# Cluster maxima of a routing-attention kernel kept in spare columns of the values' PSUM bank

## The chip, the cores and the metric

The kernel runs on one core of one Trainium2 chip. The metric is the device time of one execution in microseconds (us), as the median of the runs shown. TensorE, VectorE, ScalarE, GpSimd and SyncE appear in the profile as PE (PEld for its weight loads), DVE, ACT, POOL and SP.

## The reference

Four batches of eight heads, 768 tokens each, head width 64. Every query and key goes to the nearest of 16 centroids of its head, and a query attends only to keys with the same cluster. The result, 3072 rows of 512, passes through a feed-forward block with a softmax-gated unit and a normalisation.

```python
q_assign = np.argmax(np.einsum('bhsd,hcd->bhsc', q_n, c_n), axis=-1)
k_assign = np.argmax(np.einsum('bhsd,hcd->bhsc', k_n, c_n), axis=-1)
mask = q_assign[:, :, :, None] == k_assign[:, :, None, :]
scores = np.where(mask, scale * np.matmul(q, k.transpose(0, 1, 3, 2)), -1e9)
attn = softmax(scores)                       # with 1e-9 in the divisor
x = np.matmul(attn, v)                       # heads side by side: (3072, 512)
h = x @ w_in                                 # (3072, 1024)
solu = h * softmax(h)
out = (layernorm(solu) * g_ln) @ w_out       # (3072, 512)
```

The part that the change touches is the argmax: the maximum of 16 products per token, and the comparison with it that gives a one-hot row.

## The kernel before, in words

Each engine runs its own queue strictly in the order in which the program issues work. That order is one list of names, ORDER (lines 38 to 142), written out in full; every name is one small function. No scheduler moves anything. The tile framework under it adds the semaphore waits that the data need.

The names that matter here:

- `S3.0`, `S3.1`: the two halves of a score region on PE (line 641), 512 columns each, into one of two PSUM tiles `sb` of two banks. `E3` is the exponential of that region on ACT (line 651), from `sb` to the SBUF tile `e`.
- `V4.0`, `V4.1`: attention times values for two blocks of 128 queries of unit 4 (line 663): six matmuls of 65 columns each. All of them write the one PSUM bank `ob`. A group is two or three units (four or six blocks); it uses slots of 72 columns, so at most columns 0 to 431 of the bank's 512.
- `N1`: the normalisation of group 1 on DVE, a reciprocal (line 675) and a multiplication (line 686) that read `ob`. The first `V` of the next group waits for it, since it overwrites the bank.
- The assignment of one item (one or two pairs of heads; eleven items, `0.0`, `0.0.1`, `0.1`, `0.2`, `0.3`, `1.0`, `1.2`, `2.0`, `2.2`, `3.0`, `3.2`): `cl` multiplies with the centroids on PE, `tb` transposes the products on DVE to the SBUF tile `cst` (line 479), `mx` takes the maxima of each 16 on DVE (line 489), `oh` compares `cst` with them on DVE (line 493), `ot` transposes the one-hot rows on DVE (lines 500 and 505), and four `pl` place them in the operands of `S`, on POOL, DVE or ACT (line 531 and 529).
- The feed-forward block of 128 rows: `h` (PE, line 772, banks `hb`), `hm` (DVE, line 782, frees `hb`), `ex` (ACT), `u` (POOL or DVE), `bn` (DVE), `y` (PE, line 844, bank `mb`), `sc`. `mf` is a pair of fp32 matmuls at the start (line 614) and `wi` casts the first weights on POOL (line 580).

The maxima of an item are 12, 24 or 48 fp32 numbers per partition. They live in an SBUF tile `mx` of a pool with two buffers, written by `mx` and read once by `oh`; both are DVE instructions. Where `mx` and `oh` stand among the value products in ORDER:

```text
item   ahead of mx        between mx and oh                              behind oh
0.2    V1.1 N0            V2.0 V2.1 V3.0 V3.1                            N1
0.3    N1                 (mk)                                           V4.0 ... N2
1.0    V13.1 N6           V14.0 V14.1 V15.0 V15.1 N7 V16.0 ... V17.1     hm0.0 N8 ot1.0
1.2    V26.1 N12          -                                              V27.0
2.0    V41.1              N17 V42.0 V42.1 V43.0 V43.1                    ot2.0 N18
2.2    V53.1 N22          (sc4)                                          V54.0
3.0    V65.1              hm10.1                                         hm11.0 bn8.1 N26 V66.0
3.2    V71.1              hm12.0 hm12.1 N29 V72.0 V72.1                  hm13.0 V73.0
```

The items `0.0`, `0.0.1` and `0.1` stand ahead of the first value product.

Of the kernel before, what the change touches and what calls it, by code (L numbers as in the profile page):

```python
# [10 lines left out]
F32 = mybir.dt.float32  # L11
BF16 = mybir.dt.bfloat16
AX = mybir.AxisListType.X
# [131 lines left out]
class Weave:  # L145
# [7 lines left out]
    def add(self, name, eng, cost, key, fn, needs=(), after=(), take=None, give=None, move=0.0,  # L153
            bulk=False, lag=(0.5, 0.6)):
        assert name not in self.ops, name
        self.ops[name] = dict(fn=fn, first=[*needs, *after], take=take, give=give)
# [17 lines left out]
def kernel(  # L174
# [11 lines left out]
    nc = tc.nc  # L186
    B, H, S, D = q.shape
    NC_ = centroids.shape[1]
    assert centroids.shape[0] == H and D == 64 and NC_ == 16
    P = 128  # L190
# [4 lines left out]
    HALF = S // 2  # L195
# [7 lines left out]
    VS, VW = D + 8, D + 1  # L203
# [13 lines left out]
    pr = ctx.enter_context(tc.tile_pool(name="pr", bufs=2))  # L217
# [8 lines left out]
    add = wv.add  # L226

    def on(name, engine):
        return AWAY.get(name, engine)
# [5 lines left out]
    ob = psum.tile([P, BANK], F32, name="ob")  # L235
# [13 lines left out]
    def early(b):  # L249
        return b == 0  # L250
# [89 lines left out]
    for n in range(0, n_units, 2):  # L340
        regions_of[n] = []
        c = 0
        while c < 2 * UW:
            w = BANK if n < 2 * n_fine else 2 * BANK
            if w == 2 * BANK and ring % 2:
                w = BANK
# [13 lines left out]
    def first_of(b, p):  # L360
        return 2 * min(n for (b2, h, su), n in where.items() if b2 == b and pair_of(h) == p)
# [7 lines left out]
    raws, xts, asg, vfs = {}, {}, {}, {}  # L369
# [84 lines left out]
    def item_name(t):  # L454
        m, c0, _ = ITEMS[t]
        return "{}.{}".format(*pairs[m[0]]) + (".1" if c0 else "")
# [6 lines left out]
    def clusters(t, n):  # L463
        m, c0, L = ITEMS[t]
        b, p = pairs[n]
        for c in range(4):
            i, x = divmod(c, 2)
            w = (c_bd0[:, heads_of(p)[c0 // HALF if n == 0 else x], :] if early(b)
                 else c_bd[:, p, :])
            nc.tensor.matmul(bank_of(t, n)[c * NB:(c + 1) * NB, :L], w,  # L470
                             xts[b, p, i][:, c0 + x * L:c0 + (x + 1) * L],
                             tile_position=(0, c * NB))

    def turn_back(t, n):
        m, _, L = ITEMS[t]
        if (t, "cst") not in asg:
            asg[t, "cst"] = pr.tile([P, 2 * HALF], F32, name="cst")
        x = n - m[0]
        nc.vector.transpose(asg[t, "cst"][:, x * L:(x + 1) * L], bank_of(t, n)[:, :L])

    def wide(t):
        return len(ITEMS[t][0]) * ITEMS[t][2]

    def each(x, t):
        return x[:, :wide(t)].rearrange("p (a c) -> p a c", c=NC_)

    def assign_max(t):
        asg[t, "mx"] = pr.tile([P, 2 * HALF // NC_], F32, name="mx")
        nc.vector.reduce_max(asg[t, "mx"][:, :wide(t) // NC_], each(asg[t, "cst"], t), axis=AX)

    def assign_hot(t):
        asg[t, "oh"] = pr.tile([P, 2 * HALF], BF16, name="oh")
        nc.vector.tensor_tensor(each(asg[t, "oh"], t), each(asg[t, "cst"], t),
                                asg[t, "mx"][:, :wide(t) // NC_].unsqueeze(2)
                                .to_broadcast([P, wide(t) // NC_, NC_]), op=Alu.is_ge)

    def assign_turn(t):
        asg[t, "oht"] = pr.tile([P, 2 * HALF], BF16, name="oht")
        if not early(pairs[ITEMS[t][0][0]][0]):
            nc.vector.transpose(asg[t, "oht"][:, :wide(t)], asg[t, "oh"][:, :wide(t)])  # L500
            return

        w = wide(t)
        for x in range(2):
            nc.vector.transpose(
                asg[t, "oht"][:, :2 * w].rearrange("p (j q c) -> p j q c", j=n_t // 2, q=2)[:, :, x],
                asg[t, "oh"][:, :w].rearrange("p (k q c) -> p k q c", q=2, c=NC_)[:, :, x]
                .unsqueeze(2).to_broadcast([P, w // NB, 2, NC_]))

    def place(t, i, x, e):  # L510

        m, c0, L = ITEMS[t]
        w = len(m)
        big_, pp = home(i, *pairs[m[0]])
        r = slice((2 * i + x) * NB, (2 * i + x + 1) * NB)
        if not early(pairs[m[0]][0]):
            src = asg[t, "oht"][r, :w * L].bitcast(F32)
            src = (src.rearrange("p (g s) -> p g s", g=w).unsqueeze(2)
                   .to_broadcast([NB, w, 2, L // 2]))
            dst = big_[D:HOT, pp:pp + w, :, x * L:(x + 1) * L].bitcast(F32)  # L520
        elif m[0]:
            src = asg[t, "oht"][r, :2 * L].bitcast(F32)
            dst = big_[D:HOT, pp, x].bitcast(F32)
        else:
            src = asg[t, "oht"][r, :2 * L].bitcast(F32).rearrange("p (t c) -> p t c", c=NB)
            dst = (big_[D:HOT, pp, c0 // HALF].bitcast(F32)
                   .rearrange("p (t a c) -> p t a c", a=2, c=NB)[:, :, x])
        if e == "ACT":
            nc.scalar.copy(dst, src)
        else:  # L530
            (nc.vector if e == "DVE" else nc.gpsimd).tensor_copy(dst, src)

    def placings(t, i=None, x=None):

        return [f"pl{item_name(t)}.{j}.{y}" for j in (1, 0) for y in range(2)
                if i in (None, j) and x in (None, y)]
# [421 lines left out]
    def behind(n, what):  # L958

        if n < R:  # L960
            return []
        b, p = pairs[n - R]
        if what == "S":
            return [f"S{r}.{x}" for r in regions_with(b, p) for x in range(REG[r][2] // BANK)]
        ns = sorted({where[b, h, su] for h in heads_of(p) for su in range(n_t)})
        return [f"V{m}.{j}" for m in ns for j, (h, _) in enumerate(UNITS[m][1])
                if pair_of(h) == p]
# [11 lines left out]
    for b, p in pairs:  # L979
        n = index[b, p]  # L980
        at = first_of(b, p)
        for i in range(2):
            t, seq = f"{b}.{p}.{i}", 2 * n + i
# [42 lines left out]
            for hh in range(2):  # L1026
                for hf in range(2 if n == 0 else 1):
                    nm = f"ca{t}.{hh}.{hf}" if n == 0 else f"ca{t}.{hh}"
                    e = on(nm, "ACT" if n == 0 and i == 0 else "POOL")
                    w = HALF if n == 0 else S  # L1030
# [8 lines left out]
        t = f"{b}.{p}"  # L1039
# [11 lines left out]
    for t, (m, c0, L) in enumerate(ITEMS):  # L1051
        w, tm = wide(t) / HALF, item_name(t)
        before = item_name(t - 2) if t >= 2 else None
        for n in m:
            b, p = pairs[n]
            nm = f"cl{tm}" if n == m[0] else f"cl{b}.{p}"
            half = "xa" if n == 0 and c0 == 0 else "xt"
            tk = "m" if len(m) == 1 else f"h{n - m[0]}"
            add(nm, "PE", 0.15 + 0.635 * L / HALF, first_of(b, p) - 9,
                (lambda t=t, n=n: clusters(t, n)),  # L1060
                [f"{half}{b}.{p}.0", f"{half}{b}.{p}.1", "cb"]
                + (hb_free[n - m[0]][-1:] if len(m) > 1 else []), take=tk)
            tb = nm.replace("cl", "tb")
            nd = [nm] + ([f"oh{before}"] if before else [])
            add(tb, "DVE", 0.1 + 0.41 * L / HALF, first_of(b, p) - 20,
                (lambda t=t, n=n: turn_back(t, n)), nd, list(last_tb), give=tk)
        last_tb[:] = [nm.replace("cl", "tb")]
        at = first_of(*pairs[m[0]])
        tbs = [f"tb{tm}"] + ["tb{}.{}".format(*pairs[n]) for n in m[1:]]
        add(f"mx{tm}", "DVE", 0.16 + 0.4 * w, at - 9, (lambda t=t: assign_max(t)), tbs,  # L1070
            [f"mx{item_name(t - 1)}"] if t else [])
        add(f"oh{tm}", "DVE", 0.18 + 0.4 * w, at - 9, (lambda t=t: assign_hot(t)),
            [f"mx{tm}"] + ([f"ot{before}"] if before else []),
            [f"oh{item_name(t - 1)}"] if t else [])
        nd = placings(t - 2) if before else []
        add(f"ot{tm}", "DVE", 0.1 + 0.4 * w, at - 9, (lambda t=t: assign_turn(t)),
            [f"oh{tm}"] + nd, [f"ot{item_name(t - 1)}"] if t else [])
        bh = [x for n in m for x in behind(n, "S")]
        for j, nm in enumerate(placings(t)):
            i, x = [int(z) for z in nm[len(f"pl{tm}."):].split(".")]  # L1080
            e = on(nm, ("POOL", "DVE")[j % 2] if t < 2 else "POOL")
            w2 = w
            cost = {"POOL": 0.2 + 0.34 * w2, "DVE": 0.15 + 0.21 * w2, "ACT": 0.21 + 0.32 * w2}[e]
            add(nm, e, cost, at - 8,
                (lambda t=t, i=i, x=x, e=e: place(t, i, x, e)), [f"ot{tm}"] + bh)
        if early(pairs[m[0]][0]):
            continue
        e = on(f"bl{tm}", "POOL")
        add(f"bl{tm}", e, 0.02 + 0.36 * w if e == "POOL" else 0.05 + 0.26 * w, at - 8,
            (lambda t=t, e=e: blank(t, e)), placings(t, 1))  # L1090
# [91 lines left out]
    for f in range(n_f):  # L1182
# [20 lines left out]
        else:  # L1203
            w = 1 + twos(f)
# [150 lines left out]
```

## Time and profile before

| | |
|---|---|
| median of three runs | 221.88 us (221.68 to 222.42) |
| span of the profiled execution, first to last instruction | 220.5 us |
| median less span | 1.4 us |
| busy: PE / ACT / DVE / POOL | 211.4 / 192.8 / 185.7 / 158.8 us |
| value products into `ob` (line 663) | 1152 weight loads of 97 ns |
| `mx` (line 489) | 11 instructions, 0.35 to 0.95 us |
| `oh` (line 493) | 11 instructions, 0.36 to 1.55 us |

The profile keeps no total of its own for the profiled execution beside the span, so a change of the span is carried over to the median as it is. A row of the timeline gives the start from the beginning of the span, the length, the engine, the source line, the operation, output and input tiles with their shapes, and how many instructions of one line were joined. In brackets stands idle time of the engine ahead of the row and what ended it.

### The profile page before, as it was taken

The numbers are of one execution on the slowest core, as the hardware profiler recorded it, in microseconds if no ns is written. First come the engines' busy times: TensorE is split into PE (matmuls) and PEld (weight loads), VectorE is DVE, ScalarE is ACT, GpSimd is POOL, SyncE is SP. The second block draws the span as 40 slices with busy tenths as digits, with TensorE's granted clock in tenths as the row PEclk, the third lists the DMA queues.
The fourth block names the chain that finished last, engine by engine and source line by source line (L and its number), as shares of the span: only waits on it lengthen the run. The fifth ranks groups of instructions, "written<-read, shape, count | busy, mean of one in ns | idle before, by whom it ended". The sixth has DMA issues, their size and how long they took to land.

```text
span 220.5 us, 6292 instructions
## 1 busy us (share of the span) xinstructions
PE 211.4 (96%) x2401; PEld 148.9 (68%) x2431; DVE 185.7 (84%) x430; ACT 192.8 (87%) x245; POOL 158.8 (72%) x198
## 2 busy tenths in 40 slices
PE   7899999999999999999999999999999999999984
PEld 4567577677678776777677677666777767655442
DVE  3699979968999999896799999994888856989982
ACT  3799999999999998999999989999999888685362
POOL 3686969897898999549939997879889054456610
PEclk9999999999999999999999999999999999999999
DMA  5998999999999993999999981939584229777522
GB/s 199 394 402 259 189 175 300 126 154 259 164 154 169 190 188 62 174 248 210 153 225 162 180 184 38 171 92 209 151 173 90 72 64 168 154 120 170 163 94 100
DMA packets 120911, 38.33 MB, mean 174 GB/s; under 512 B 109993, under 2 KB 116401, under 8 KB 120881
## 3 DMA queue, kind: packets, MB, share of 16 engines
q1 hardware_dynamic: 120448, 37.40, 81.7%
q10 hardware_dynamic: 432, 0.52, 0.7%
q8 instruction: 19, 0.31, 0.6%
q14 instruction: 12, 0.09, 0.2%
HBM read 23.11 MB, written 6.29 MB: 133 GB/s over the span
## 4 chain that ended last, share of the span: by engine, by line
PE 72%; DVE 10%; DMA 6%; POOL 5%; issue 3%; ACT 2%; SPq 1%; DVEq 0%; ACTq 0%; POOLq 0%
PE sb L641 22%; PE hb L772 16%; PE mb L844 15%; PE ob L663 12%; DMA w_st<-in_moe_w_in_dram 4%; PE hb L470 3%; DMA raw<-in_q_dram 2%; DVE w_st L782 2%; PE hb L396 2%; DVE xt L421 2%; DVE bs L816 2%; POOL kbig L441 1%; PE mb L470 1%; POOL w_in_sb L580 1%; POOL v L556 1%
## 5 line engine op out<-in xcount | busy, mean ns | idle before, releaser
L651 ACT ACTIVATE e<-sb 128x1024 bf16<-128x1024 f32 x144 | 139.9, 1024 | 8.9 <-PE sb L641 8.1
L641 PE MATMUL sb<-qbig,kbig 80*128 80x256 bf16 (+3 forms) x648 | 83.8, 261 | 1.3 <-ACT e L651 1.0
L641 PEld LDWEIGHTS <-kbig 80*128 80x128 bf16 (+1 forms) x648 | 62.9, 119 | 25.4 <-issue 8.6
L805 POOL TENSOR_TENSOR u<-e_sb,w_st 128x1024 bf16<-128x1024 bf16 x21 | 45.1, 2145 | 20.0 <-ACT e_sb L798 13.3
L663 PEld LDWEIGHTS <-e 128*128 128x128 bf16 x1152 | 48.6, 97 | 10.4 <-DVE x L686 0.6
L663 PE MATMUL ob<-v,e 128*128 128x65 bf16 x1140 | 51.4, 193 | 0.2
L772 PE MATMUL hb<-w_in_sb,xT 128*128 128x512 bf16 x173 | 50.6, 379 | 0.9 <-POOL v L1323 0.3
L844 PE MATMUL mb<-w_out_c,uT 128*128 128x512 bf16 x165 | 45.5, 379 | 1.2 <-DVE y L858 0.4
L816 DVE BATCH_NORM_STATS2 bs<-u 128x6 f32<-128x512 bf16 x48 | 31.6, 680 | 1.1 <-POOL u L805 1.1
L798 ACT ACTIVATE e_sb<-w_st,nmax 128x1024 bf16<-128x1024 f32 (+1 forms) x25 | 27.8, 1113 | 3.2 <-DVE w_st L782 1.8
L439 POOL CAST qbig<-xt 64x768 bf16<-64x768 f32 (+1 forms) x31 | 25.7, 830 | 6.5 <-PE ob L663 2.7
L441 POOL TENSOR_SCALAR kbig<-xt 64x768 bf16<-64x768 f32 (+1 forms) x32 | 27.6, 865 | 2.4 <-DVE xt L409 0.8
L840 POOL TENSOR_TENSOR alpha<-var,halves 128x1 f32<-128x1 f32 x24 | 15.3, 638 | 12.6 <-DVE var L823 8.0
L421 DVE STREAM_TRANSPOSE xt<-raw 128x768 f32<-128x768 f32 x24 | 22.5, 959 | 0.1
L844 PEld LDWEIGHTS <-uT 128*128 128x128 bf16 x176 | 15.2, 97 | 10.2 <-issue 0.8
L772 PEld LDWEIGHTS <-xT 128*128 128x128 bf16 x192 | 15.8, 98 | 8.8 <-issue 0.6
L686 DVE TENSOR_TENSOR x<-ob,den 128x256 bf16<-128x256 f32 (+2 forms) x40 | 19.0, 474 | 1.4
L782 DVE TENSOR_SCALAR_CACHE_REDUCE w_st<-hb 128x512 f32<-128x512 f32 x24 | 16.3, 680 | 3.8 <-PE hb L772 3.7
L782 DVE TENSOR_SCALAR_CACHE_REDUCE w_st<-hb,nmax 128x512 f32<-128x512 f32 x24 | 17.8, 740 | 1.9 <-PE hb L772 1.5
L856 ACT ACTIVATE y<-mb,alpha 128x512 f32<-128x512 f32 x15 | 10.3, 685 | 6.5 <-POOL alpha L840 3.6
L675 DVE RECIPROCAL den<-ob 128x4 f32<-128x4 f32 (+2 forms) x40 | 7.1, 178 | 10.4 <-PE ob L663 10.1
L556 POOL CAST v<-vf 128x384 bf16<-128x384 f32 x22 | 10.9, 504 | 3.3 <-DMA vf<-in_v_dram 2.6
(109 smaller groups left out, 202.6 us busy)
## 6 DMA issues: line engine op xcount, KB each, us to landing
vf<-in_v_dram SPq DMA_DIRECT2D x16, 384.0 KB, 5.3
out_dram<-y SPq DMA_DIRECT2D x23, 256.0 KB, 2.5
raw<-in_k_dram SPq DMA_DIRECT2D x26, 192.0 KB, 4.6
raw<-in_q_dram SPq DMA_DIRECT2D x24, 192.0 KB, 5.1
w_g<-in_moe_w_out_dram SPq DMA_DIRECT2D x4, 512.0 KB, 8.7
w_st<-in_moe_w_in_dram SPq DMA_DIRECT2D x4, 512.0 KB, 8.0
raw<-in_q_dram SPq DMA_DIRECT2D x3, 384.0 KB, 6.6
raw<-in_k_dram SPq DMA_DIRECT2D x3, 384.0 KB, 7.6
```

What stands on the lines that cost most here:

```text
L421: nc.vector.transpose(xts[b, p, i][:], raw_of(b, p, i))
L439: (nc.vector if e == "DVE" else nc.gpsimd).tensor_copy(dst, src)
L441: (nc.vector if e == "DVE" else nc.gpsimd).tensor_scalar(dst, src, scalar1=inv_C, scalar2=1.0, op0=Alu.mult, op1=Alu.mult)
L641: nc.tensor.matmul(reg[:, c:c + wd], kb[u, pp, side_of(h), keys], qb[u, pp, side_of(h), su * P:su * P + wd])
L651: nc.scalar.activation(es[r][:, :w], src, Act.Exp, scale=exp_scale, bias=-exp_scale)
L663: nc.tensor.matmul(ops_of(group_of[n])[:, s, :VW], es[r][:, c0:c0 + P], v1[index[b, pair_of(h)] % R][:, side_of(h), kt, :VW], start=(kt == ...
L772: nc.tensor.matmul(hb[f2][:], xTs[f][:, dc, :], w_in_sb[:, dc, f2 * BANK:(f2 + 1) * BANK], start=(dc == 0), stop=(dc == n_dc - 1))
L782: nc.vector.tensor_scalar(ff[f, "h"][:, f2 * BANK:(f2 + 1) * BANK], hb[f2][:], scalar1=-1.0, scalar2=nmax[:, f2 - 1:f2] if f2 else 3.0e38, ...
L798: nc.scalar.activation(ff[f, "e"][:, cols(f, f2)], ff[f, "h"][:, cols(f, f2)], Act.Exp, bias=ff[f, "nmax"][:, n_ff2 - 1:], scale=-1.0, acc ...
L805: (nc.vector if e == "DVE" else nc.gpsimd).tensor_tensor(ff[f, "u"][:, cols(f, f2)], ff[f, "e"][:, cols(f, f2)], ff[f, "h"][:, cols(f, f2) ...
L816: nc.vector.bn_stats(ff[f, "bs"][:, f2, :], ff[f, "u"][:, f2 * BANK:(f2 + 1) * BANK])
L844: nc.tensor.matmul(y_of(f, x), ff[f, "uT"][:, fc, :], w_out_c[:, fc, parts_of(f, x)], start=(fc == 0), stop=(fc == n_fc - 1))
```

## The change

The maxima are written to columns 432 and up of the bank `ob` (fp32, at most 48 columns, to 479), which no value product uses, and the comparison reads them there. There is one place for them in place of two buffers, so `mx` of an item is declared to stand behind `oh` of the item before. ORDER is not touched.

```diff
+    def highest(t):
+
+        return ob[:, 6 * VS:6 * VS + wide(t) // NC_]
+
     def assign_max(t):
-        asg[t, "mx"] = pr.tile([P, 2 * HALF // NC_], F32, name="mx")
-        nc.vector.reduce_max(asg[t, "mx"][:, :wide(t) // NC_], each(asg[t, "cst"], t), axis=AX)
+        nc.vector.reduce_max(highest(t), each(asg[t, "cst"], t), axis=AX)
 
     def assign_hot(t):
         asg[t, "oh"] = pr.tile([P, 2 * HALF], BF16, name="oh")
         nc.vector.tensor_tensor(each(asg[t, "oh"], t), each(asg[t, "cst"], t),
-                                asg[t, "mx"][:, :wide(t) // NC_].unsqueeze(2)
+                                highest(t).unsqueeze(2)
                                 .to_broadcast([P, wide(t) // NC_, NC_]), op=Alu.is_ge)
...
-        add(f"mx{tm}", "DVE", 0.16 + 0.4 * w, at - 9, (lambda t=t: assign_max(t)), tbs,
-            [f"mx{item_name(t - 1)}"] if t else [])
+        add(f"mx{tm}", "DVE", 0.16 + 0.4 * w, at - 9, (lambda t=t: assign_max(t)),
+            tbs + ([f"oh{item_name(t - 1)}"] if t else ["xa0.0.1"]))
```

The instructions of every engine are the same in number, kind and order. What differs is the tile name and the semaphores that they wait for. On DVE, around `mx` and `oh` of item `0.2` (the second row is the multiplication of `N0`, the third `mx`, the seventh `oh`), before:

```order
L675 RECIPROCAL den<-ob 128x4 [waits PE_49]
L686 TENSOR_TENSOR x<-ob,den 128x2x2x64 [waits DVE_49]
L489 TENSOR_REDUCE mx<-cst 128x24
L409 COPY xt<-hb_92 128x384 [waits PE_49,Activation_49,Pool_49]
L589 TENSOR_SCALAR g_ln_111<-mb 128x8 [waits PE_49]
L409 COPY xt<-hb_93 128x384 [waits PE_49,Activation_49]
L493 TENSOR_TENSOR oh<-cst,mx 128x384 [waits DVE_49]
```

And of the change, on the same engine and at the same place:

```order
L678 RECIPROCAL den<-ob 128x4 [waits PE_49]
L689 TENSOR_TENSOR x<-ob,den 128x2x2x64 [waits DVE_49]
L492 TENSOR_REDUCE ob<-cst 128x24 [waits DVE_49]
L409 COPY xt<-hb_92 128x384 [waits PE_49,Activation_49,Pool_49]
L592 TENSOR_SCALAR g_ln_111<-mb 128x8 [waits PE_49]
L409 COPY xt<-hb_93 128x384 [waits PE_49,Activation_49]
L496 TENSOR_TENSOR oh<-cst,ob 128x384 [waits DVE_49,PE_49]
```

Nothing moved; the comparison has a wait for PE that it had not. On DVE around item `2.0` (`mx`, an `as`, the two of `N17`, `oh`, `ot`, the first of `N18`), before:

```order
L489 TENSOR_REDUCE mx<-cst 128x48 [waits DVE_49]
L835 TENSOR_SCALAR es_1699<-esum 128x1 [waits Activation_49]
L675 RECIPROCAL den<-ob 128x6 [waits PE_49]
L686 TENSOR_TENSOR x<-ob,den 128x6x64 [waits DVE_49]
L493 TENSOR_TENSOR oh<-cst,mx 128x768
L500 STREAM_TRANSPOSE oht<-oh 128x768 [waits DVE_49]
L675 RECIPROCAL den<-ob 128x4 [waits PE_49]
```

And of the change, again DVE around item `2.0`:

```order
L492 TENSOR_REDUCE ob<-cst 128x48 [waits DVE_49,PE_49]
L838 TENSOR_SCALAR es_1691<-esum 128x1 [waits Activation_49]
L678 RECIPROCAL den<-ob 128x6 [waits DVE_49]
L689 TENSOR_TENSOR x<-ob,den 128x6x64 [waits DVE_49]
L496 TENSOR_TENSOR oh<-cst,ob 128x768 [waits PE_49]
L503 STREAM_TRANSPOSE oht<-oh 128x768 [waits DVE_49]
L678 RECIPROCAL den<-ob 128x4
```

The waits for PE went from the two reciprocals to `mx` and `oh` ahead of them. In the built program the wait values say which instruction is meant: `oh` of an item waits for the last value product issued ahead of it (`V3.1` for `0.2`, `V17.1` for `1.0`, `V43.1` for `2.0`, `V72.1` for `3.2`), `mx` of `3.0` for `V65.1`, and a value product issued behind `mx` or `oh` waits for that one (`V4.0` for `oh0.3`, `V14.0` for `mx1.0`, `V27.0` for `oh1.2`, `V54.0` for `oh2.2`, `V73.0` for `oh3.2`).

## The prediction, made before the change was run

> **What bounds the kernel now.** First the slices of DVE and ACT (40 of 5.5 us, busy tenths) and the chain of work that ended last, on the page:
>
> ```profile
> DVE  3699979968999999896799999994888856989982
> ACT  3799999999999998999999989999999888685362
> PE 72%; DVE 10%; DMA 6%; POOL 5%; issue 3%; ACT 2%; SPq 1%; DVEq 0%; ACTq 0%; POOLq 0%
> ```
>
> The reader is to see that no engine has room: PE carries 72% of the chain, and ACT and DVE are at 9 tenths in most slices up to 160 us, where all eleven items lie. A stop of PE there reaches ACT as soon as the next score region is late. The rest of the argument is the timeline, engine by engine, around each `mx` and `oh`.
>
> **The change part by part.** It removes no instruction and adds none. [...]
>
> **The rule of the waits.** A `mx` or `oh` now waits for every value product issued ahead of it, and every value product for the `mx` or `oh` issued ahead of it; the wait values in the program say so. [...]
>
> **A, items 0.2 and 0.3.**
>
> ```profile
> 19.99 0.53 PE L663 MATMUL ob<-v,e 128*128 128x65 bf16 x12
> 19.54 0.69 DVE L493 TENSOR_TENSOR oh<-cst,mx 128x384 bf16<-128x384 f32 x1
> 25.70 0.57 DVE L493 TENSOR_TENSOR oh<-cst,mx 128x384 bf16<-128x384 f32 x1
> 24.92 0.88 PEld L663 LDWEIGHTS <-e 128*128 128x128 bf16 x24
> 26.24 0.60 PE L641 MATMUL sb<-qbig,kbig 80*128 80x256 bf16 x4 [0.32 <-ACT e L651]
> 26.68 1.02 PE L614 MATMUL hb<-y,fold 128*128 128x512 f32 x2
> 26.63 3.76 ACT L651 ACTIVATE e<-sb 128x1024 bf16<-128x1024 f32 x4
> ```
>
> `oh0.2` began at 19.54; the products up to `V3.1` end at 19.99 + 0.53 = 20.52, so it starts 0.98 later. DVE has work without a gap from there to `oh0.3` (11 instructions lie between the two), so `oh0.3` ends not at 25.70 + 0.57 = 26.27 but near 27.13, taking 0.57 for both comparisons. `V4.0`, loaded at 24.92, now waits for that: PE stops for 2.2 us. Behind it stand `S12` (26.24), `mf` (26.68 to 27.70) and `S13`, as long as `S12`. `S12` had waited 0.32 for ACT, so it starts 1.9 later, ends at 28.7, `mf` follows to 29.6 and `S13` to 30.2. ACT's four exponentials come every 0.92 us: `E12` at 27.55 and `E13` at 28.47. `E13` now starts at 30.2. ACT, back to back here, loses **1.7 us** (between 1.2, by `E12` alone, and 2.2, the whole stop of PE).
>
> **B, item 1.0.**
>
> ```profile
> 41.02 0.95 DVE L489 TENSOR_REDUCE mx<-cst 128x48 f32<-128x768 f32 x1
> 40.39 0.51 PEld L663 LDWEIGHTS <-e 128*128 128x128 bf16 x12
> 42.81 0.38 PE L772 MATMUL hb<-w_in_sb,xT 128*128 128x512 bf16 x1 [0.33 <-POOL v L1323]
> 45.10 0.34 PE L663 MATMUL ob<-v,e 128*128 128x65 bf16 x6
> 42.65 0.95 DVE L493 TENSOR_TENSOR oh<-cst,mx 128x768 bf16<-128x768 f32 x1
> 43.53 0.69 DVE L782 TENSOR_SCALAR_CACHE_REDUCE w_st<-hb 128x512 f32<-128x512 f32 x1
> 45.48 0.18 DVE L675 RECIPROCAL den<-ob 128x4 f32<-128x4 f32 x1 [1.25 <-PE ob L663]
> 45.70 0.42 DVE L686 TENSOR_TENSOR x<-ob,den 128x256 bf16<-128x256 f32 x1
> 46.49 0.39 PEld L663 LDWEIGHTS <-e 128*128 128x128 bf16 x8
> ```
>
> `V14.0` (40.39) waits for `mx1.0`, which ends at 41.97: 1.58. PE's wait of 0.33 for POOL's cast at 42.81 takes some back, leaving 1.25. `V17.1` then ends at 45.44 + 1.25 = 46.69. Only there may `oh1.0` start, which used to run in DVE's 1.25 of idle time together with `hm0.0`; the two take 43.53 + 0.69 - 42.65 = 1.57, and `N8` starts at 48.26 in place of 45.48. It ends 2.78 later, at 48.90, and `V18.0`, which had stood at 46.49, follows: **2.4 us** (1.25 if `N8` were free, 2.8 if all of it counts).
>
> **C, item 1.2.**
>
> ```profile
> 62.58 1.55 DVE L493 TENSOR_TENSOR oh<-cst,mx 128x768 bf16<-128x768 f32 x1
> 61.64 0.51 PEld L663 LDWEIGHTS <-e 128*128 128x128 bf16 x12
> 63.87 1.02 ACT L651 ACTIVATE e<-sb 128x1024 bf16<-128x1024 f32 x1 [0.17 <-PE sb L641]
> ```
>
> `V27.0` (61.64) waits for `oh1.2`. That lasts 0.95, if POOL lets it (below), and ends at 63.53: 1.9. The next exponential, `E45`, already waited for PE's scores, so nothing hides it: **1.9 us** (2.5 with a comparison of 1.55).
>
> **D, item 2.0.**
>
> ```profile
> 87.56 1.48 DVE L493 TENSOR_TENSOR oh<-cst,mx 128x768 bf16<-128x768 f32 x1
> 89.07 0.98 DVE L500 STREAM_TRANSPOSE oht<-oh 128x768 bf16<-128x768 bf16 x1
> 90.52 0.18 DVE L675 RECIPROCAL den<-ob 128x4 f32<-128x4 f32 x1 [0.47 <-PE ob L663]
> 91.19 1.16 DVE L531 COPY kbig<-oht 32x768 f32<-32x768 f32 x1
> 92.38 0.55 DVE L531 COPY qbig<-oht 32x768 f32<-32x768 f32 x1
> 92.29 0.43 PEld L663 LDWEIGHTS <-e 128*128 128x128 bf16 x6
> ```
>
> `oh2.0` and `ot2.0` used the time in which DVE waited for `V43.1`. Now they start where `N18` started, at 90.52, and push it by 0.95 + 0.98 = 1.93, to end at 93.09; `V44.0` (92.29) is 0.8 late. DVE is without a gap up to `N19`, so that is 1.9 late unless the copy of 1.16, whose like takes 0.55, runs undisturbed 1.9 later: **1.3 us** (0.8 to 1.9).
>
> **E, item 2.2.**
>
> ```profile
> 111.78 0.95 DVE L493 TENSOR_TENSOR oh<-cst,mx 128x768 bf16<-128x768 f32 x1
> 110.31 0.33 PEld L663 LDWEIGHTS <-e 128*128 128x128 bf16 x6
> 113.58 1.02 ACT L651 ACTIVATE e<-sb 128x1024 bf16<-128x1024 f32 x1 [0.39 <-PE sb L641]
> ```
>
> `V54.0` (110.31) waits for the end of `oh2.2` at 112.73, and ACT had no lead over PE: **2.4 us**.
>
> **F, item 3.0.**
>
> ```profile
> 127.91 0.94 DVE L489 TENSOR_REDUCE mx<-cst 128x48 f32<-128x768 f32 x1
> 131.05 0.71 PE L663 MATMUL ob<-v,e 128*128 128x65 bf16 x18
> 129.44 1.37 DVE L493 TENSOR_TENSOR oh<-cst,mx 128x768 bf16<-128x768 f32 x1
> 132.11 0.18 DVE L675 RECIPROCAL den<-ob 128x6 f32<-128x6 f32 x1
> 132.32 0.56 DVE L686 TENSOR_TENSOR x<-ob,den 128x384 bf16<-128x384 f32 x1
> 133.23 0.51 PEld L663 LDWEIGHTS <-e 128*128 128x128 bf16 x12
> ```
>
> `mx3.0` (127.91) now waits for `V65.1`, which ends at 131.76. Behind it on DVE stand `hm10.1`, `oh3.0`, `hm11.0` and `bn8.1`, then `N26`. That took 132.11 - 127.91 = 4.20, and with a comparison of 0.95 and no wait inside about 3.6. `N26` starts at 135.4, 3.3 late, and ends at 136.15; `V66.0` (133.23) is **2.9 us** late (3.3 at most). `hm10.1` also frees the bank for `h11.1.0`, an earlier part of the same stop.
>
> **G, item 3.2.**
>
> ```profile
> 147.39 0.95 DVE L493 TENSOR_TENSOR oh<-cst,mx 128x768 bf16<-128x768 f32 x1
> 148.15 0.53 PE L663 MATMUL ob<-v,e 128*128 128x65 bf16 x12
> 149.49 0.60 PEld L663 LDWEIGHTS <-e 128*128 128x128 bf16 x15
> ```
>
> `oh3.2` starts at 148.68 and ends at 149.63; `V73.0` (149.49) is **0.1 us** late. `hm13.0` behind it is 1.3 late, the upper end.
>
> The three items ahead of `V0.0` meet no product: nothing.
>
> **Where the maxima lie.** The nearest rows are comparisons of DVE with an operand in PSUM or without: `x<-ob,den` of 256 elements (PSUM) took 0.42, `oh` of 768 (SBUF) 0.95, `x<-ob,den` of 384 0.56. From 256 to 384 an element costs 1.1 ns, from there to 768 1.0; the memory does not show. I take nothing; 0.03 either way on 22 instructions is 0.7 us.
>
> **The port.** The same comparison of 768 elements took 0.95 three times and 1.37, 1.48 and 1.55 elsewhere. I take 0.95, the nearer and more frequent row, everywhere; with the long ones C, D and F grow by 0.6, 0.5 and 0.4. [...]
>
> **The sum.** 1.7 + 2.4 + 1.9 + 1.3 + 2.4 + 2.9 + 0.1 = 12.7 us. Each term is the lateness of PE or ACT against its own place, so they add, as long as the engines stay full between them. The span goes from 220.5 to 233.2, and the median of 221.88 to **234.6**.
>
> **The rivals.** (1) Stops that only PE suffers are made good. At C and E DVE loses nothing; if it runs ahead there and its work is what holds PE later (the chain has 10% on DVE), those 4.3 are given back: 8.4, 230.3 us. Against it: ACT's waits for PE just behind both. (2) Everything counts on its own engine: 2.2 + 2.8 + 2.5 + 1.9 + 2.4 + 3.3 + 1.3 = 16.4, 238.3 us. For it: DVE's slices of 9. (3) The other side: the waits are met by the time they are reached, and only the shorter comparisons remain. At `oh1.2`, `oh2.0` and `oh3.0`, where DVE is full, that saves 0.6 + 0.5 + 0.4: 220.4 us. It decides from the point at which a bank is handed over sooner than the rows say, for instance if waits were kept by columns. Against it stand the wait values and `V27.0`, loaded 0.94 ahead of `oh1.2`'s start. (4) The change does not bring the waits that it says, and nothing moves: 221.9.
>
> **How the numbers follow.** The forecast has 0.58, with 232.4 to 237 as its own range from the bounds of A to G; rival 1 has 0.20, rival 2 0.18, rivals 3 and 4 0.02 each. To leave out no more than 2 in 10 the range takes in most of rivals 1 and 2: 229.5 to 238.5. Slower by over 0.3%, which is about what a measurement of this kernel can tell from no change, has 0.96; faster and within 0.3% have 0.02 each.
>
> **What the profile of the change would show.** The multiplications of `V4.0`, `V14.0`, `V27.0`, `V54.0` released by line 496 or 492 on DVE; DVE idle ahead of `oh1.0`, `oh2.0` and `mx3.0`, released by PE on `ob`; all comparisons of 768 at 0.95; ACT with two idle stretches of some 2 us at C and E. Against me would be a busy sum as before with the span less than 8 us longer (the stops overlap), DVE idle but ACT not, or comparisons of 1.0 and more with no POOL beside them.

## The result, and the profile after

The changed kernel took **238.29 us** in the median of 4 runs (237.24 to 239.55) against 222.15 of the kernel before beside it (221.68 to 222.46): 1.0723 times, 95% interval 1.0676 to 1.0770, or 16.1 us slower. Forecast were 234.6 with a range of 229.5 to 238.5. (In the first and the eleventh experiment one run each fell into a stretch in which the chip gave TensorE some 0.66 of its clock throughout, 321.39 and 314.26 us; they are left out below.)

The profiled execution has a span of 235.9 us and took 237.69, 15.4 more span than before. The page's slices of 5.9 us, and its chain:

```profile
DVE  2688878578959998596884975997699765889983
ACT  3799799889969998979947995899989987786461
PEclk9999999999999999999988999999999999999998
PE 75%; DVE 12%; ACT 4%; DMA 3%; issue 3%; SPq 1%; DVEq 0%; ACTq 0%
```

DVE, which stood at 9 in most slices, has holes. `PEclk`, the granted clock, has two slices at 8 in the middle and one at the very end; before, it was full. The costliest group of ACT on the two pages, before and then after (busy, mean, idle ahead and its releaser):

```profile
L651 ACT ACTIVATE e<-sb 128x1024 bf16<-128x1024 f32 x144 | 139.9, 1024 | 8.9 <-PE sb L641 8.1
```

```profile
L654 ACT ACTIVATE e<-sb 128x1024 bf16<-128x1024 f32 x144 | 140.6, 1024 | 22.3 <-PE sb L644 20.2
```

The exponentials work as long as before and wait for PE's scores 12.1 us longer. Where the waits lie is read from the value products on PE, timeline of after (start, length, and in brackets the wait of PE and its releaser), at A, B (two rows), C, D, E and F (two rows, the first for the product `h11.1.0`):

```profile
27.71 0.89 PE L666 MATMUL ob<-v,e 128*128 128x65 bf16 x24 [2.24 <-DVE oh L496]
...
44.02 0.52 PE L666 MATMUL ob<-v,e 128*128 128x65 bf16 x12 [1.38 <-DVE ob L492]
...
50.68 0.71 PE L666 MATMUL ob<-v,e 128*128 128x65 bf16 x18 [0.90 <-DVE x L689]
...
67.67 0.54 PE L666 MATMUL ob<-v,e 128*128 128x65 bf16 x12 [1.68 <-DVE oh L496]
...
99.24 0.34 PE L666 MATMUL ob<-v,e 128*128 128x65 bf16 x6 [0.41 <-DVE x L689]
...
120.98 0.34 PE L666 MATMUL ob<-v,e 128*128 128x65 bf16 x6 [2.20 <-DVE oh L496]
...
145.66 0.59 PE L775 MATMUL hb<-w_in_sb,xT 128*128 128x512 bf16 x2 [1.71 <-DVE w_st L785]
...
148.44 0.54 PE L666 MATMUL ob<-v,e 128*128 128x65 bf16 x12 [0.87 <-DVE x L689]
```

Four of them are released by the very `oh` or `mx` that the prediction names. At D, at F and at the second row of B the product waits for the normalisation (line 689), because DVE had itself waited ahead of it. At F most of PE's standstill comes earlier, in the 1.71 us that `h11.1.0` waits for `hm10.1`; the prediction named that wait as "an earlier part of the same stop". DVE's timeline of after has those waits, at `oh0.2`, `oh1.0`, `oh2.0`, `mx3.0` and `oh3.2`:

```profile
20.91 0.56 DVE L496 TENSOR_TENSOR oh<-cst,ob 128x384 bf16<-128x384 f32 x1 [0.81 <-PE ob L666]
...
48.51 0.95 DVE L496 TENSOR_TENSOR oh<-cst,ob 128x768 bf16<-128x768 f32 x1 [2.26 <-PE ob L666]
...
96.69 0.96 DVE L496 TENSOR_TENSOR oh<-cst,ob 128x768 bf16<-128x768 f32 x1 [2.79 <-PE ob L666]
...
143.99 0.96 DVE L492 TENSOR_REDUCE ob<-cst 128x48 f32<-128x768 f32 x1 [3.80 <-PE ob L666]
...
163.99 0.95 DVE L496 TENSOR_TENSOR oh<-cst,ob 128x768 bf16<-128x768 f32 x1 [1.23 <-PE ob L666]
```

To size each stop, the start of every value product was set against its start before. The lateness goes up in steps; within a step it swings (at A 2.67 at `V5`, 1.98 from `V8` on), and between two steps it stays within a few hundredths:

| stop, between | forecast | lateness ahead | behind | step | alone (experiments) |
|---|---|---|---|---|---|
| start, ahead of `V0` | - | 0 | 0.35 | 0.35 | |
| A, `V3` and `V6` | 1.7 | 0.35 | 1.98 | 1.63 | 1.63 |
| B, `V14` and `V19` | 2.4 | 1.98 | 4.08 | 2.10 | 2.10 |
| C, `V26` and `V30` | 1.9 | 4.08 | 5.80 | 1.72 | 1.72 |
| D, `V41` and `V47` | 1.3 | 5.80 | 8.20 | 2.40 | 2.04 |
| E, `V53` and `V56` | 2.4 | 8.20 | 12.20 | 4.00 | 2.45, with half clock 3.8 to 4.0 |
| F, `V65` and `V70` | 2.9 | 12.20 | 15.28 | 3.08 | 3.08 |
| G, `V73` and `V78` | 0.1 | 15.28 | 15.38 | 0.10 | |

The steps make 15.38, the growth of the span. The 0.35 at the start, ahead of every value product, is no stop: in the traces of the experiments below the same place lies between 0.06 earlier and 0.70 later than in the one trace of before (2.11 in a run with half clock there). Forecast were 12.7. A, B, C, F and G are within 0.3 us of the forecast; E (1.6 more) and D (1.1 more) hold the miss. The last column anticipates the runs below in which one stop stands alone.

At E, the granted clock in stretches of 3.41 us (start and end, length, PE busy with its instructions, granted clock, DMA share, GB/s), after:

```profile
115.26:118.67 3.41, 3.41 (x52) 1.00 1.04 164
118.67:122.08 3.41, 1.16 (x12) 1.00 0.73 190
122.08:125.50 3.42, 3.42 (x29) 0.50 1.20 241
125.50:128.91 3.41, 3.36 (x39) 1.00 1.16 184
```

Just behind the stop PE works 3.41 us at half clock. That brings ACT a second wait, the second row below (timeline of after):

```profile
123.11 1.02 ACT L654 ACTIVATE e<-sb 128x1024 bf16<-128x1024 f32 x1 [2.73 <-PE sb L644]
125.77 1.94 ACT L654 ACTIVATE e<-sb 128x1024 bf16<-128x1024 f32 x2 [1.63 <-PE sb L644]
```

The 2.20 us of the stop are E as forecast; the 1.6 us behind it come from the clock. The mean clocks of the four runs were 0.993, 0.990, 0.986 and 0.986. One stretch of 3.41 us at half clock in 236 costs 0.007 of the mean, and the end of the span up to 0.003 (1.2 us at 0.50 in this trace, with PE idle), so every run had one or two.

### The profile page after: what moved, and what is told of

The parts are those of the page before. It is cut to its first block, busy times and chain, and to the rows that moved or that the text cites. A ratio compares the mean times of both kernels' runs of the same rounds, so it can differ in the third digit from the quotient of the medians.

```text
span 235.9 us, 6291 instructions
## 1 busy us (share of the span) xinstructions
PE 214.3 (91%) x2401; PEld 149.4 (63%) x2431; DVE 184.1 (78%) x430; ACT 193.8 (82%) x245; POOL 155.6 (66%) x198
## 4 chain that ended last, share of the span: by engine, by line
PE 75%; DVE 12%; ACT 4%; DMA 3%; issue 3%; SPq 1%; DVEq 0%; ACTq 0%
PE sb L644 23%; PE hb L775 16%; PE mb L847 15%; PE ob L666 14%; PE hb L470 3%; ACT e L654 3%; DMA raw<-in_q_dram 3%; DVE oh L496 2%; DVE ob L492 1%; PE hb L396 1%; DVE qbig L534 1%; DVE cst L479 1%; DVE w_st L785 1%; DVE x L689 1%; DVE y L861 1%
## 5 line engine op out<-in xcount | busy, mean ns | idle before, releaser
L644 PE MATMUL sb<-qbig,kbig 80*128 80x256 bf16 (+3 forms) x648 | 84.7, 263 | 1.7 <-DVE qbig L534 0.7
L439 POOL CAST qbig<-xt 64x768 bf16<-64x768 f32 (+1 forms) x31 | 24.8, 803 | 7.2 <-DVE xt L421 4.1
L441 POOL TENSOR_SCALAR kbig<-xt 64x768 bf16<-64x768 f32 (+1 forms) x32 | 25.6, 802 | 3.3 <-PE mb L847 0.8
L843 POOL TENSOR_TENSOR alpha<-var,halves 128x1 f32<-128x1 f32 x24 | 14.6, 612 | 12.7 <-DVE var L826 8.0
L534 POOL COPY kbig<-oht 32x768 f32<-32x768 f32 (+2 forms) x14 | 10.5, 750 | 13.2 <-DVE oht L503 5.4
```

What stands on the lines that cost most here:

```text
L441: (nc.vector if e == "DVE" else nc.gpsimd).tensor_scalar(dst, src, scalar1=inv_C, scalar2=1.0, op0=Alu.mult, op1=Alu.mult)
L644: nc.tensor.matmul(reg[:, c:c + wd], kb[u, pp, side_of(h), keys], qb[u, pp, side_of(h), su * P:su * P + wd])
```

## The experiments

**My theory**: the waits bring the whole loss, stop by stop; the stops add, and a stop of 2.2 us can bring half clock besides. **Rivals**: the place of the maxima (PSUM operands, or the long comparisons that the prediction takes up under "The port") has a part in it; the stops overlap or are given back (rival 1 of the prediction); half clock at E has nothing to do with the stop.

**The waits alone.** The maxima go back to SBUF, and small instructions take on the waits:

```diff
+    AHEAD = ("oh0.2", "oh1.0", "oh2.0", "mx3.0", "oh3.2")
+    BEHIND = ("oh0.3", "mx1.0", "oh1.0", "oh1.2", "oh2.0", "oh2.2", "oh3.0", "oh3.2")
+    def touch(name, those):
+        if name in those:
+            nc.vector.memset(ob[:, 511:], 0.0)
```

> The maxima lie in SBUF as before the change, but a one-word memset of DVE to an unused column of ob stands ahead of oh0.2, oh1.0, oh2.0, mx3.0 and oh3.2 and behind oh0.3, mx1.0, oh1.0, oh1.2, oh2.0, oh2.2, oh3.0 and oh3.2: 13 small instructions that take on the waits of the change and nothing else. If the waits carry the loss: as slow as the change, 16 us over before, plus 13 memsets of some 0.1 us each at most, so +15 to +18 us, with PE's stop of about 2.2 us in item 2.2. If the place of the maxima or the port carries a part of it: at least 2 us less than the change, under +14 us.

Measured: 239.29, 240.58 and 242.47 us beside 222.24, 1.084 times (1.0785 to 1.0895), +18.7 us by the ratio. The mean clocks were 0.993, 0.986 and 0.972, one to four half stretches. That is 0.7 above the expected interval, and the run of one stretch is 2 us over the changed kernel's run of one stretch (237.24). Spread over the 13 memsets that is 0.16 for each; the one trace, which is of the run at 0.66 of the clock, gives them 59 ns each, so they explain less than half of the 2 us by their own length, and the rest stays open. Nor can that trace show PE's stop of 2.2 us at full clock. The waits without the new place bring at least the whole loss; under +14 us was the rival's.

**The place without the waits.** The maxima of five items (10 of the 22 instructions) lie in PSUM where no wait comes of it:

```diff
+    HOMES = {"0.0": ob, "0.0.1": ob, "0.1": ob, "1.0": hb[1], "2.0": hb[0]}
-... S27.1 V15.1 h0.0.0 h0.0.1 N7 E26 ... E30 oh1.0 hm0.0 N8
+... S27.1 V15.1 h0.0.0 h0.0.1 N7 oh1.0 E26 ... E30 hm0.0 N8
```

> The maxima of items 0.0, 0.0.1, 0.1, 1.0 and 2.0 lie in PSUM (the first three in ob ahead of any product, 1.0 and 2.0 in the two banks of hb), the others in SBUF; oh1.0 is moved ahead in the order so that no comparison or maximum waits for a product. 10 of 22 instructions then read or write PSUM with none of the waits. If the place is worth nothing by itself and the shorter comparison ahead of N18 is eaten by the wait for the value product behind it: within 0.3 us of before (+0.1 us for 8 ns on each of ten). If the freed port is a gain: the comparison oh2.0 falls from 1.48 to 0.95 and the time by 0.5 us or more. If PSUM operands are dear: over +0.7 us.

Measured: 222.28 us in 12 runs beside 222.24, 1.0001 times (0.9984 to 1.0018): no change. DVE's timeline of this kernel at `oh2.0`, the next `N18`, and the copy behind it:

```profile
87.11 0.94 DVE L502 TENSOR_TENSOR oh<-cst,hb 128x768 bf16<-128x768 f32 x1
...
90.07 0.18 DVE L684 RECIPROCAL den<-ob 128x4 f32<-128x4 f32 x1 [1.00 <-PE ob L672]
...
90.74 0.62 DVE L540 COPY kbig<-oht 32x768 f32<-32x768 f32 x1
```

The comparison fell from 1.48 to 0.94 and POOL's cast beside it from 1.53 to 0.82, so the shorter rows are real. The copy behind `N18` fell from 1.16 to 0.62 as well. But the wait for the value product ahead of `N18` grew from 0.47 to 1.00: what DVE saves, it waits. So rival 3 had a true premise and no gain at `oh2.0`; the other two long comparisons, `oh1.2` and `oh3.0`, were not tried without the waits.

**Only item 2.2 (E).** Here and in the next runs `HOMES` holds the named items, and the others keep their maxima in SBUF:

```diff
+    HOMES = {"2.2": ob}
```

> Only item 2.2 keeps its maxima in ob, the other ten keep them in SBUF: stop E alone. By the stop alone +2.4 us; by the stop and a half clock behind it +4.0 us, with a stretch of 3.4 us at a granted clock of 0.5 that begins about 1 us behind the stop. If stops compound (each dearer because the others stand ahead of it): well under 2.4 us.

Measured: 224.66, 224.69, 225.15 and, in the profiled run, 227.81 us beside 222.24; 1.0155 times (1.0104 to 1.0207). Three runs at a clock of 1.00 give the stop alone: +2.45. The profiled one had two stretches of half clock, one while the first loads came in (8.20 us) and one behind the stop:

```profile
4.79:8.20 3.41, 1.67 (x13) 1.00 0.96 319
8.20:11.61 3.41, 3.41 (x25) 0.50 1.07 398
...
110.60:114.01 3.41, 1.69 (x20) 1.00 0.90 141
114.01:117.43 3.42, 2.94 (x16) 0.50 0.89 268
117.43:120.84 3.41, 3.41 (x47) 1.00 1.24 224
```

PE's stop is 2.20 us in the trace as in the changed kernel, and the step of the value products there 3.76. One stop, one kernel, and two prices. The half clock came in one run of four, which the theory had not said.

**The whole change, the product moved past the wait:**

```diff
-... S84.1 V54.0 h8.1.0 h8.1.1 ex7.0 E83 S85.0 S85.1 E84 E85 pl2.2.0.1 pl2.2.1.1 V54.1
+... S84.1 h8.1.0 h8.1.1 ex7.0 E83 S85.0 S85.1 E84 E85 pl2.2.0.1 pl2.2.1.1 V54.0 V54.1
```

> The whole change, with the first product of pair 54 moved in PE's order from ahead of S85.0 to behind S85.1, so that two scores and a history product run while oh2.2 ends. If E's 4.0 us are a stop of 2.2 us and a half clock that the stop brings: the stop falls to under 1 us, no half clock follows, and the time is 3 us less than the change (about +13 us over before). If the half clock has nothing to do with that stop: about 1.4 us less than the change, with a stretch of half clock as before.

Measured: 234.50 us (233.78 to 235.33) beside 222.24, 1.0558 times (1.0528 to 1.0589), 3.8 us less than the change had taken. Three runs had a clock of 1.00, the fourth (235.33) 0.993. PE's and ACT's timelines of this kernel:

```profile
121.07 0.89 PE L672 MATMUL ob<-v,e 128*128 128x65 bf16 x24 [0.87 <-DVE oh L502]
```

```profile
122.92 1.94 ACT L660 ACTIVATE e<-sb 128x1024 bf16<-128x1024 f32 x2 [1.54 <-PE sb L650]
```

The stop is 0.87 and ACT's wait 1.54, with the clock full behind it; E's step is 1.05 in place of 4.00. That is 2.95 of the 3.8 us; the rest can come from the median of the change, two of whose four runs had a second stretch of half clock.

**Only item 2.0 (D).**

```diff
+    HOMES = {"2.0": ob}
```

> Only item 2.0 keeps its maxima in ob: D alone. By the prediction's step (oh2.0 and ot2.0 pushed behind the value product, 1.9 us, of which the undisturbed copy to kbig gives 0.6 back) +1.3 us. By the trace of the change, where D came to 2.4 us because the copies were slow again at their new place and DVE lost a few tenths more: +2.2 to +2.5 us, with the copy to kbig or qbig again over 0.8 us.

Measured: 224.37 us (6 runs) beside 222.31, 1.0089 times (1.0059 to 1.0119), +2.1. DVE's timeline of this kernel has the two copies behind `N18`:

```profile
93.02 0.83 DVE L540 COPY kbig<-oht 32x768 f32<-32x768 f32 x1
93.88 1.07 DVE L540 COPY qbig<-oht 32x768 f32<-32x768 f32 x1
```

Before, they took 1.16 and 0.55, together 1.71; now 1.90. POOL's own cast to `kbig` (1.02 us at 93.52) came later as well and lies mostly beside the second copy instead of the first. The step of the value products is 2.04.

**Only item 3.0 (F).**

```diff
+    HOMES = {"3.0": ob}
```

> Only item 3.0 keeps its maxima in ob: F alone. If the stops add: +2.9 us, as in the change, with mx3.0 held back by 3.5 to 4 us. If the other stops had already shifted DVE against PE and so set F's size: more than 0.5 us off 2.9. If a half clock follows the stop of 1.7 us: up to 1.6 us more in single runs.

Measured: 225.39 us (224.62 to 225.63) beside 222.31, 1.0127 times (1.0075 to 1.0179), +3.1; `mx3.0` is held back by 3.80 us, PE stands still for 1.71 us ahead of `h11.1.0` and for 0.87 ahead of `V66.0`, all as in the changed kernel, and no run had half clock (0.999 and above).

**Only item 1.2 (C).**

```diff
+    HOMES = {"1.2": ob}
```

> Only item 1.2 keeps its maxima in ob: C alone, a stop of PE with no instruction of DVE held back. If it isn't made good (my step): +1.7 to +1.9 us, the lateness of V78 equal to that of V30. If such stops are given back (rival 1 of the prediction): under +0.5 us.

Measured: 224.00 us (9 runs) beside 222.31, 1.0074 times (1.0050 to 1.0097), +1.7. The lateness is 1.72 more behind the stop than ahead of it, and from `V29` to `V95` it stays as it is. ACT's timeline of this kernel:

```profile
65.39 4.82 ACT L660 ACTIVATE e<-sb 128x1024 bf16<-128x1024 f32 x5 [2.04 <-PE sb L650]
```

Nothing is given back, though DVE lost nothing here. Rival 1 falls.

**Only items 0.2 and 0.3 (A).**

```diff
+    HOMES = {"0.2": ob, "0.3": ob}
```

> Only items 0.2 and 0.3 keep their maxima in ob: A alone. If the stops add: +1.6 us, as in the change. The stop of PE is as long as in item 2.2 (2.2 us); if such a stop can bring the half clock anywhere, single runs lie up to 1.6 us higher, with 3.4 us at a clock of 0.5 behind 25 us.

Measured: 224.19 us (10 runs) beside 222.31, 1.0099 times (1.0070 to 1.0128). Seven runs at a clock of 0.998 and above have a median of 223.96, +1.65; three at 0.992 lie at 225.22, 225.51 and 225.70, another 1.55 higher. The half clock is not bound to item 2.2. (The trace is of a run without it, so that the stretch lies behind this stop is taken from the mean clock and not seen.)

**A longer stop.**

```diff
     def assign_hot(t):
+        for _ in range(2 if item_name(t) == "2.2" else 1):
-        nc.vector.tensor_tensor(each(asg[t, "oh"], t), each(asg[t, "cst"], t),
+            nc.vector.tensor_tensor(each(asg[t, "oh"], t), each(asg[t, "cst"], t),
```

> Only item 2.2 keeps its maxima in ob, and its comparison is done twice, one behind the other, so that PE's stop there grows from 2.3 us to some 3.2 us. Without a change of clock: +3.3 us over before (2.4 and another 0.9). If half clock comes by the length of the stop and not by chance: in every run, some +4.8 us, mean clock near 0.992. If it comes by how the stop falls into a window of 3.4 us that runs by itself, a chance that grows with the stop's length: in most runs but not in all, more often than in the kernel with the single comparison; the runs then lie in two groups some 1.5 us apart.

Measured: 227.45 us (6 runs) beside 222.01, 1.0250 times (1.0215 to 1.0285), +5.4. All six runs had the half clock (0.992, one 0.982), 0.6 us dearer than expected. Six of six don't tell "by the length" from a chance that grows with it. PE's row has the stop, and the stretches the clock:

```profile
113.97 0.41 PE L673 MATMUL ob<-v,e 128*128 128x65 bf16 x6 [3.19 <-DVE oh L503]
```

```profile
110.69:114.10 3.41, 0.22 (x6) 1.00 0.77 114
114.10:117.52 3.42, 3.42 (x29) 0.50 1.14 309
```

**Only item 2.2 once more**, the same kernel as above, for the count.

> The kernel of only item 2.2 once more, for the count: of its first four runs one had the half clock and was 1.5 to 3 us slower than the others. If that is chance by the phase of a window: a few of these runs have it, at a mean clock near 0.992 and 1.5 us over the rest, which lie at +2.4 us over before.

Measured: five of six runs at 0.990 to 0.992 (225.84 to 227.29, median 226.37) and one at 1.00 (224.69) beside 222.01; 1.0180 times (1.0140 to 1.0220). Half clock costs 1.7 us here. Five are more than the expected few. With the runs of above, 6 of 10 had it behind a stop of 2.20 us, at A 3 of 10, behind 3.19 us 6 of 6, and in the 22 runs of only C, D, F or B counted here, with stops of 1.7 us and less, none.

**Only item 1.0 (B).**

```diff
+    HOMES = {"1.0": ob}
```

> Only item 1.0 keeps its maxima in ob: B alone, the one term not yet tried by itself. If the stops add: +2.1 us, as in the change. By the prediction's bounds 1.25 to 2.8 us. No stop of PE here is over 1.4 us, so no run has the half clock.

Measured: 224.94, 225.09 and 225.36 us beside 222.01, 1.0139 times (1.0103 to 1.0174), +3.1, over the bounds. In the trace the step between `V14` and `V19` is 2.10, as in the change; a further 0.23 comes at `V42`, and 0.70 stood ahead of `V0`, where the loads begin. Another part lies in the trace of before: its wait of 0.33 for POOL's cast at 42.81 is missing in six of the nine other traces in which item 1.0 is not held back, and their products from `V16` on come 0.3 to 0.4 us earlier. (In the other three the wait is 0.15, 0.46 and 0.73.) So against a kernel without that wait the step is near 2.5, an estimate from 2.10 and the 0.39 of five traces; with the 0.23 that makes 2.7 of the 3.1, and the prediction, which let that wait take 0.33 off, leaned on something that comes and goes.

**Work for PE in the stop**, in the kernel with the longer stop:

```diff
-        for c, n, x, kt in chunks_in(n0, c0 + half * BANK):
+        for c, n, x, kt in chunks_in(n0, c0 + half * BANK) * (9 if (r, half) == (84, 1) else 1):
```

> As in the kernel with the doubled comparison of item 2.2, but PE does the two multiplications of S84.1 nine times over ahead of V54.0, some 1.8 us of work whose result is the same, while it waits. V54.0 goes on at the same time as there (by DVE's second comparison), and E84, late by about 1 us, is still ended long ahead of E85. If the half clock comes by how little PE works in a window of 3.41 us: that window is then busy for about 2.0 us of 3.41, over the half, no run has the half clock, and the time is +3.3 us over before, 1.5 to 2 us under the kernel without the filling. If it comes by the wait itself (or by anything that follows the lateness of ACT and DVE): +5.2 us, as there. If the repeated multiplications hold up anything else: over +3.6 us with no half clock.

Measured: five of six runs at a clock of 0.992 (226.88 to 227.66) and one at 1.00 (225.39) beside 221.90; 1.0214 times (1.0179 to 1.0248). The expectation of no half clock failed; the one run without it has +3.5 us, near the +3.3 of the stop alone. PE's row behind the filling, and the stretches:

```profile
114.01 0.34 PE L673 MATMUL ob<-v,e 128*128 128x65 bf16 x6 [1.44 <-DVE oh L503]
```

```profile
111.04:114.45 3.41, 1.91 (x22) 1.00 0.91 239
114.45:117.87 3.42, 3.42 (x26) 0.50 1.20 228
```

PE was busy for 1.91 of 3.41 us, over half, and stood still for no more than 1.44, less than at C or F, and half clock came all the same. In the kernel of only A it was less busy and none came:

```profile
25.95:29.36 3.41, 1.59 (x29) 1.00 0.95 146
29.36:32.77 3.41, 3.09 (x41) 1.00 1.01 209
```

So the busy share of a stretch does not decide alone. It goes far, though. The half clock lies on a grid of 3.41 us: the two starts in the first run of only item 2.2, 8.20 and 114.01, are 105.81 us or 31 stretches apart, and in the changed kernel the one at 122.08 and the one at 234.7, near the end of the span, 33. In the changed kernel no stretch of the grid with PE busy for 1.94 us or more was followed by half clock. Of the stretches read at the stops and at both ends, those with 0.22 (the longer stop), 1.16 and 1.36 (the changed kernel, E and the end) and 1.29 (only item 2.2 once more) were; of the others 1.67, 1.69 and 1.91 were, and 1.59, 1.70, 1.73 and 1.86 were not.

The filling was score products, which use 80 of PE's 128 rows (80*128 in their rows of the trace, 128*128 in those of the value products). If their time (1.53 of the 1.91) counts by the rows, 1.34 us are left, and in the stretch of only A 1.36 (0.60 of its 1.59 were scores); counted so, the four others behind which half clock came at E (in the changed kernel and in the runs of it alone) lie at 1.29 and less, and those at C and F, without it, at 1.47 and more. But the stretch at the start of the first run of only item 2.2 (4.79 to 8.20, shown there) does not fit: its 1.67 us are fp32 products on all 128 rows (128*128 and 128*32 at that place in the trace of before), and half clock followed. The count by rows was made afterwards and wasn't tried by itself. What exactly sets off the half clock stays open.

## Why the prediction was right, and where it was off

**The rule of the waits: right.** Product, maximum and comparison of this program wait for each other by the bank, in columns that never meet: in the trace of after DVE waits 0.81 to 3.80 us for the products ahead of five of them, and PE 1.38 to 2.24 us ahead of four products. Terms worked out by it came within 0.1 us (A), 0.3 (B), 0.2 (C), 0.2 (F) and 0.0 (G) of their steps. The waits alone are at least as slow as the change; the place alone, tried on 10 of the 22 instructions, costs nothing that can be told from 0 (0.9984 to 1.0018).

**The sum: right in kind.** The stops add. Each one's step alone is its step in the whole change, but for D and, by the half clock, E; none is given back by the end of the program. Rival 1 (20%) is out by the run of only C. Rival 2 (18%) gave 238.3 us, all but the time measured, yet not by its reasons: its terms A 2.2, B 2.8 and C 2.5 did not come (1.63, 2.10, 1.72).

**E: the failed term.** "ACT had no lead over PE: 2.4 us" holds to a tenth, in the three runs of only item 2.2 at full clock (+2.45). What the step left out is that PE, after it has stood still, may come back slower: 3.41 us at 0.50 of the clock, and 1.6 us more in the profiled run. The prediction counted every stretch behind a stop at the durations of before, and so put this at nothing without a reason. The traces show the length (3.41 us) and the clock (0.50), and the runs that it comes in some and not in others of the same kernel, 6 of 10 for only item 2.2; PE need not be idle for a whole stretch, since it was busy for 1.16 of 3.41 us ahead of the half clock of the changed kernel. The last column of the table has both prices.

**D: mis-sized.** "Unless the copy of 1.16, whose like takes 0.55, runs undisturbed 1.9 later: 1.3 us (0.8 to 1.9)". The copy did fall, to 0.83, but its neighbour rose to 1.07, and POOL's cast came later too and now lay mostly beside that one (99.71 to 100.73 in the change, the copies at 99.22 and 100.08; that the cast makes them longer is read from their times, and a kernel without it wasn't tried). Alone D was 2.04, 0.1 over the upper bound. In the whole change another 0.37 comes ahead of `V42`: PE's wait there for DVE's `y` grew from 0.36 to 0.74, and DVE had stood idle for 0.51 ahead of a small `var` instruction (0.14 before). Its releaser isn't plain in the trace, the same place lost 0.2 in the runs of only A and only B, and the cause stays open.

**Where the maxima lie: right.** The prediction took nothing, give or take 0.7; `mx` of 768 went from a mean of 948 to 957 ns, and `oh` of 768 takes 952 where the three short ones had taken 946 to 948. On 22 instructions that is 0.2 us at most.

**The long comparisons: right in their rows, and worth nothing.** No run shows a port. The rows of before show three comparisons of 1.37 to 1.55 us with both operands in SBUF and a cast of POOL beside them; two others with a cast beside them took 0.95. Those of after show 0.95 with the maxima in PSUM. The 0.95 of the terms, "if POOL lets it" at C, was the author's estimate from three rows of before. The group of after (busy, mean ns, idle before):

```profile
L496 DVE TENSOR_TENSOR oh<-cst,ob 128x768 bf16<-128x768 f32 x6 | 5.7, 952 | 6.3 <-PE ob L666 6.3
```

Six comparisons at 952 on the mean, none long. DVE's busy time fell from 185.7 to 184.1 us and POOL's from 158.8 to 155.6, and the run of the place alone shows, for `oh2.0`, that no time follows.

**The range** held the time with 0.2 us to spare, and by luck. The forecast's own part of it, 232.4 to 237, was missed by 1.3 us: 16.1 us were measured for 12.7. (The bounds of A to F alone add up to its upper end, 15.1 us over before; G's 1.3 is not in it.) What it lacked at the top was the half clock and D, which the part added for rival 2 happened to cover.

## What to carry to other kernels

Unused columns of the PSUM bank `ob` were no free storage: by the wait values all its writers and readers stand in line, and DVE and PE, which had run side by side there, waited for each other (DVE up to 3.80 us at one place, PE up to 2.24). Price such a wait at its place, by the next engine in the chain: where that one had no lead, the lateness stayed (1.72 us from `V29` to `V95` with only C), and the stops at different places added (15.03 of the 15.38 us of the table). Then ask two more things of each stop: whether PE does so little around it that it comes back at half clock (here by chance, behind stops of 2.17 us and more, and behind one of 1.44 us that score products had filled; `V54.0` moved past the wait took 2.95 us off the step), and whether a slow row that is to be escaped will move along (at D the copy fell from 1.16 to 0.83 us, and its neighbour rose from 0.55 to 1.07).

## What the runs showed of the hardware

- Half clock on TensorE behind a stop in the middle of a busy program: 3.41 us at 0.50, worth 1.55 to 1.7 us, in 20 of 34 runs of kernels with a stop of 2.17 to 3.19 us or two (counted by a mean clock under 0.994, which doesn't say where the stretch lay), in none of 22 with stops of up to 1.7 us, and in 1 of 58 runs of the kernel before. With the stop filled down to 1.44 us it came in 5 of 6. The three runs of the waits alone, which had it too, are not counted, since no trace at full clock shows their stops. Of the same kernel some runs have it and some don't, so its times lie in two groups.
- Of the stretches of 3.41 us read in the traces, the four with PE busy for 0.22, 1.16, 1.29 and 1.36 us were followed by half clock, and in the changed kernel none with 1.94 or more; one with 1.91 was, and one with 1.59 was not.
- A comparison of 768 with the maxima in PSUM took 952 ns on the mean of six; with both operands in SBUF, three took 946 to 948 ns and three, beside a cast of POOL, 0.4 to 0.6 us more. At `oh1.0` of the kernel before it was POOL's cast that was long instead (42.75, 1.52 us; the same cast at 87.40 took 0.82), and at `oh3.2` two casts took 2.50 together.
